# Wide token chunks: a token group moved between the first step's products, one addition per turn moved to GpSimd, the last step in another order

## The chip, the cores and the metric

One core of a Trainium2 chip runs the whole program. The metric is the device time of one execution in microseconds; of several executions the median is taken. Before the change it is 2312.31 us (three runs, 2310.08 to 2313.94).

## The reference

Two stages, in fp32, on x of 8 x 3008 x 256 (batch, tokens, channels). The first filters along the tokens: a real FFT over the 3008 tokens, a complex 256 x 256 channel mixing, a soft threshold, and the inverse FFT. The second is a mixer block:

```
X  = rfft(x, axis=1)
Yr = shrink(Xr @ w_r - Xi @ w_i + b_r)      # shrink: sign(v) * max(|v| - 0.01, 0)
Yi = shrink(Xr @ w_i + Xi @ w_r + b_i)
x  = irfft(Yr + 1j*Yi)                      # 8 x 3008 x 256

h   = relu(x.T @ w_tok1) @ w_tok2           # tokens: 3008 -> 256 -> 3008, per batch
u   = x + h.T
out = u + relu(u @ w_ch1) @ w_ch2           # channels: 256 -> 1536 -> 256
```

## The kernel before, in words

The eight batches are worked on in five units (one, one, two, two, two batches). The transforms, the mixing and the token layer of a unit run beside the channel layers of the unit before it, up to about 905 us; this part is the same in both kernels. What is changed lies behind it, in `channel7` (line 1193).

**u in groups.** u is made in token groups of 376 or 470 tokens (four or five sets of 94). `half_u(g, ct)` makes one half of a group, that is one of two 128-channel blocks: six products with the second token weight (tiles gh, gl, wt; `mm3` writes a value as the sum of two fp32r numbers, high and remainder, and takes three products for one), then the products with the inverse transform's tile b, one for each set of 94 tokens, all into one PSUM bank, here bank z. ScalarE copies the bank into uf, the tile that keeps u (line 975). After the second half `load_group` issues two loads for the next group on SP: wt (line 924) and b (line 946), each with one buffer.

**Channel layers in wide chunks.** From unit 1 on the tokens go in chunks of 1024 (the first of a unit has 960 or 896); these are 21 wide chunks, `ns`. In them both channel layers are computed by a seven-product scheme for 2 x 2 blocks (Strassen, in Winograd's form): u is cut in quarters (channel block by token half: u11, u12, u21, u22, which are also the places of the output sums), and each weight in 2 x 2 blocks of 128 x 128. A chunk takes six steps p, each with two of the twelve hidden blocks. A step has seven products of the first layer, N1 to N7, and seven of the second, O1 to O7; each product is three matmuls (`mm3`) with the half chunk's 512 columns moving. The O of a step run in the next step, between that step's N: `step(new, old, beside)` walks a written list of names. TensorE keeps the order that the code writes (class `InOrder`); for the other engines the compiler's scheduler fixes each queue's order when the program is built.

```
ORDER = "O1 N1 N5 O3 N6 N3 N2 N7 O5 O2 N4 O6 O4 O7"   # line 1359
TURN  = "O1 N1 N5 O5 N6 N3 N2 N7 O3 O2 N4 O6 O4 O7"   # the old step was its chunk's last
LAST  = "O1 O5 O3 O2 O6 O4 O7"                        # no new step is left
```

**Banks.** The N use three PSUM banks in turn, X (sx in the profile), W (sw) and Y (sy), and add into them: N1, N6, N7 and N4 use X, N5 and N3 use W, N2 uses Y. Between them ScalarE copies banks out (lines 1245, 1269), VectorE adds across banks (line 1216) and takes maxima with differences (line 1219). From these come the seven operands `op` of the second layer: the high part on ScalarE (line 1249), the remainder on VectorE for b11 and b22 and on GpSimd for the five others (line 1216). N4 waits for VectorE's addition into W to have read X; the next N5 waits for the b22 remainder to have read W.

The O use the banks L1, L5, L6, L7 (tile l), in which the six steps of a chunk add up, and Y (O3, O4) and z (O2), which VectorE empties into uf in every step. So O3 of a step writes Y, VectorE adds it to u12, and only then N2 may write Y.

**The turn.** In a chunk's last step the sums are finished in the step that belongs to the next chunk already. `fin` (tile t) starts as ScalarE's copy of L1; VectorE adds L6 to it (`o6`), VectorE adds fin to u12, VectorE adds L7 to fin (`o7`), GpSimd adds that to u21 and to u22, and `store` issues the chunk's output on SP. Around a turn GpSimd and ScalarE also prepare the next chunk's quarters (`sums_u`, `operand`).

**Where the groups go.** `when` (line 1400) says at which place of which step the half-groups of the next chunk stand. For the second wide chunk (two groups, four halves) they stand behind N1 of step 1 and behind the steps 1, 2 and 3 of the first wide chunk. In the first wide step, which has no old step, nothing stands between the N.

**The end.** The last chunk's last O run with no new step beside them. There o5 adds L5 to u12 and to u22, o3 and o4 empty Y twice, o6 and o7 add fin on VectorE to u12 and u21 and on GpSimd to u22, and L7 to u21 and u22; the output leaves in four stores on SP.

Of the kernel before, what the change touches and what calls it, by code (L numbers as in the profile page):

```python
# [17 lines left out]
B, N, C = 8, 3008, 256  # L18
N1, N2 = 47, 64
# [118 lines left out]
def tile_kernel(ctx: ExitStack, tc: tile.TileContext, io):  # L138
    nc = tc.nc
    V, S, G, PE, DMA, PUT = nc.vector, nc.scalar, nc.gpsimd, nc.tensor, nc.sync, nc.scalar  # L140
# [66 lines left out]
    def mm3(out, wh, wl, xh, xl, start, stop, more=False):  # L207
        PE.matmul(out, lhsT=wh, rhs=xh, start=start, stop=False, skip_group_check=more)  # L208
        PE.matmul(out, lhsT=wh, rhs=xl, start=False, stop=False, skip_group_check=more)  # L209
        PE.matmul(out, lhsT=wl, rhs=xh, start=False, stop=stop, skip_group_check=more)  # L210
# [674 lines left out]
    outv = io["out"].rearrange("(t p) b n -> b p t n", p=128)  # L885
# [3 lines left out]
    for u, bs in enumerate(UNITS):  # L889
        total, at = N * len(bs), 0  # L890
# [15 lines left out]
    for u, at, cw in chunks:  # L906
        mine = []
# [47 lines left out]
                ufs[m] = wc["uf"].tile([128, 2, CW7 if cw > CW else CW], F32, name="uf", bufs=3)  # L955
        return c0, c1, found

    def half_u(g, ct):
        u, b, s0, k = groups[g]
        gh, gl = gts[u]  # L960
        w, b2 = wts[g], b2s[g]
        c0, c1, found = home(g)
        n = c1 - c0
        cs = slice(ct * 128, (ct + 1) * 128)
        pt = wc["banks"]["z"] if "banks" in wc else bank("pu")
        for jt in range(2):
            mm3(pt[:, :n], gh[:, jt, b, cs], gl[:, jt, b, cs], w[:, jt, :n], w[:, 2 + jt, :n], jt == 0, False)
        for s in range(k):
            PE.matmul(pt[:, s * TOKS:(s + 1) * TOKS], lhsT=b2[:, s, cs], rhs=g2[:, 0 if s0 + s == 0 else 1], start=False, stop=s == k - 1)
        if g == 0:  # L970
            us[0] = [wc["wk2"].tile([128, 2, CW], F32R, name=k, bufs=1) for k in ("uh", "ul")] if ct == 0 else us[0]
            S.copy(out=us[0][0][:, ct, :n], in_=pt[:, :n])
        for m, at, cw in found:
            lo, hi = max(at, c0), min(at + cw, c1)
            S.copy(out=ufs[m][:, ct, lo - at:hi - at], in_=pt[:, lo - c0:hi - c0])
        if g == 0:
            V.tensor_tensor(out=us[0][1][:, ct, :n], in0=ufs[0][:, ct, :n], in1=us[0][0][:, ct, :n].bitcast(F32), op=ALU.subtract)
        if ct:
            del wts[g], b2s[g]
# [198 lines left out]
    def left(layer, p, i):  # L1178
        if i in MADE:
            return [wc["ws" if layer == 1 else "ws2"][:, p, MADE[i], k] for k in range(2)]  # L1180
        row, t = KEPT[i]
        if layer == 1:
            return [wc["w1"][:, k, t, (2 * p + row) * 128:(2 * p + row + 1) * 128] for k in range(2)]
        return [wc[name][:, 2 * p + t, row * 128:(row + 1) * 128] for name in ("w2h", "w2l")]
# [8 lines left out]
    def channel7(ns):  # L1193
# [7 lines left out]
        total = {k: ps2.tile([128, 512], F32, tag="l%d" % k, name="l") for k in (1, 5, 6, 7)}  # L1201
        banks = wc["banks"] = {k: bank("s" + k) for k in ("x", "w", "y", "z")}
        coming, pins = {}, {}

        def piece(g, ct):
            def f():
                half_u(g, ct)
                if ct:
                    load_group(g + 1)
            return f  # L1210

        half = NF // 2
        ADD, SUB, MAX = ALU.add, ALU.subtract, ALU.max

        def add(out, in0, in1, eng, op=ADD):
            eng.tensor_tensor(out=out, in0=in0, in1=in1, op=op)  # L1216
# [11 lines left out]
        def two(old, i):  # L1228
            n, p, h, ops = old
            op = ops[SECOND[i]]  # L1230
            if p == half - 1 and (i == 2 or i == 3 and n < ns[-1]):
                mm3(total[{2: 1, 3: 5}[i]][:, :h], *left(2, p, i), op[:, 0], op[:, 1], False, True, True)
            elif i in total:
                mm3(total[i][:, :h], *left(2, p, i), op[:, 0], op[:, 1], p == 0, p == half - 1)
            else:
                mm3(banks["z" if i == 2 else "y"][:, :h], *left(2, p, i), op[:, 0], op[:, 1], True, True)
# [60 lines left out]
        def of_second(old):  # L1297
            n, p, h, ops = old
            u11, u12, u21, u22 = quarters(n)
            L = {k: t[:, :h] for k, t in total.items()}  # L1300
            Y = banks["y"][:, :h]
            last = p == half - 1
            fin = spare(n) if last else None

            def o1(after=None):
                if after:
                    with tc.issue_after(after.ins):
                        S.copy(out=fin, in_=L[1])
                else:
                    S.copy(out=fin, in_=L[1])  # L1310

            def o3():
                add(u12, L[5] if last and n < ns[-1] else Y, u12, V)

            def o4():
                add(u21, Y, u21, V)
                if n == ns[-1] and last:
                    add(u21, fin, u21, V)

            def o5():  # L1320
                if n == ns[-1]:
                    add(u12, L[5], u12, V)
                add(u22, L[5], u22, V)

            def o2():
                add(u11, L[1] if last else banks["z"][:, :h], u11, V)

            def o6():
                add(fin, L[6], fin, V)
                if n == ns[-1]:  # L1330
                    add(u22, fin, u22, G)
                add(u12, fin, u12, V)

            def o7():
                if n == ns[-1]:
                    add(u21, L[7], u21, V)
                    add(u22, L[7], u22, V)
                    return
                add(fin, L[7], fin, V)
                add(u21, fin, u21, G)  # L1340
                add(u22, fin, u22, G)
                store(n)

            found = {("O", 3): o3, ("O", 4): o4, ("O", 2): o2}
            if last:
                found.update({"l1": o1, "l5": o5, ("O", 6): o6, ("O", 7): o7})
            return found

        def store(n, parts=((slice(0, 2), 0), (slice(0, 2), 1))):
            u, at, cw = chunks[n]  # L1350
            h = cw // 2
            uf = us[n][0]
            for t, k in parts:
                for b, bi in enumerate(UNITS[u]):
                    lo, hi = max(at + k * h, b * N), min(at + (k + 1) * h, (b + 1) * N)
                    if lo < hi:
                        DMA.dma_start(out=outv[bi][:, t, lo - b * N:hi - b * N], in_=uf[:, t, lo - at:hi - at])

        ORDER = "O1 N1 N5 O3 N6 N3 N2 N7 O5 O2 N4 O6 O4 O7".split()

        TURN = "O1 N1 N5 O5 N6 N3 N2 N7 O3 O2 N4 O6 O4 O7".split()

        LAST = "O1 O5 O3 O2 O6 O4 O7".split()

        def step(new, old, beside):
            then = of_second(old) if old else {}
# [33 lines left out]
        when = {}  # L1400
        for m in ns[1:]:
            mine = needs[m]
            if m == ns[1]:
                spots = [(ns[0], p) for p in ['N5', 'N7', (1, 'N1'), 1, 2, 3][-2 * len(mine):]]
            elif len(mine) == 2:
                spots = [(m - 2, half - 1), (m - 1, 0), (m - 1, 1), (m - 1, 2)]
            else:
                spots = [(m - 2, half - 2), (m - 2, half - 1), (m - 1, 0), (m - 1, 1), (m - 1, 2), (m - 1, 3)]
            for spot, half_g in zip(spots, [(g, ct) for g in mine for ct in range(2)]):
                when.setdefault(spot, []).append(half_g)  # L1410
        old = None
        for n in ns:
            for p in range(half):
                h = chunks[n][2] // 2
                new = n, p, h, {k: tail.tile([128, 2, CW], F32R, tag="op", name="op", bufs=9)[:, :, :h] for k in ("b11", "b22", "t1", "b21", "t2", "t4", "t3")}
                beside = {}
                if p == half - 1 and n < ns[-1]:
                    beside = {at: [operand(n + 1, k, {'b22': 'b11', 'b21': 't1'}.get(k)) for k in ks] for at, ks in {'N1': ('t1',), 'N5': ('t2',), 'N7': ('b22',), 'O2': ('b21', 't3', 't4')}.items()}
                for at in ("N1",):
                    if (n, (p, at)) in when:  # L1420
                        beside[at] = [piece(*when[n, (p, at)].pop())]
                if not old:
                    beside = {at: [piece(*when[n, at].pop())] for at in ("N5", "N7") if (n, at) in when}
                step(new, old, beside)
                old = new
                if p == half - 2 and n < ns[-1]:
                    sums_u(n + 1)
                    operand(n + 1, "b11", 'b11')()
                for g, ct in when.get((n, p), ()):
                    piece(g, ct)()  # L1430
        step(None, old, {})
        for part in ((0, 1), (1, 1), (1, 0), (0, 0)):
            store(ns[-1], ((slice(part[0], part[0] + 1), part[1]),))

    def run(gen):
        for _ in gen:
# [81 lines left out]
```

## Time and profile before

| what | before |
|---|---|
| median of three runs | 2312.31 us |
| the profiled execution, its own time | 2313.52 us |
| its span | 2311.7 us |
| granted TensorE clock, mean | 0.997 |
| first wide step begins (first product into sx) | 905.57 us |
| turns (VectorE's addition of fin to u12) | 20, the first at 981.42, the last at 2251.00 us |
| GpSimd busy from 917 to 927 / in an ordinary turn, 1449.7 to 1461.6 | 5.35 of 10.0 / 9.19 of 11.9 us |

Lines of the profile read thus: the start in us from the span's start and the duration in us; the engine (PE is TensorE, DVE VectorE, ACT ScalarE, POOL GpSimd, SPq the queue of SyncE, which issues transfers), the line of the kernel, the operation, what it writes and reads (`sx<-ub,w`), its shape, and how many were merged. In brackets stands the idle time of the engine just before, and who ended it. A waits view has one line for each pair: the waiting engine and line, who was waited for, the us in total, how often, and the longest. Matmul ends are modelled, so distances are taken from start to start. Line 134 is that of the `InOrder` helper, so all products of the wide part carry it: they are told apart by their tiles.

### The profile page before, as it was taken

The page shows a single profiled execution, that of the slowest core. Times are in us where ns is not written, and L with a number is a line of the kernel's source. Part 1 is how long each engine was busy: PE and PEld are TensorE (multiplying, and loading weights), DVE is VectorE, ACT ScalarE, POOL GpSimd, SP SyncE. Part 2 cuts the span into 40 slices and gives each one's busy share as a digit, 9 for nine tenths or more (in the row PEclk, how much of TensorE's full clock was granted, in tenths as well). Part 3 has the DMA queues.
Part 4 walks back from the last instruction along what each step waited for, and adds up shares of the span by engine and source line. Part 5 has one row for each costly group of instructions (what it writes and reads, how often), then busy time and mean ns, then how long its engine had stood idle before and what let it go on. Part 6 is the DMA issues. An engine that isn't in the chain of part 4 may idle for free.

```text
span 2311.7 us, 34801 instructions
## 1 busy us (share of the span) xinstructions
PE 2273.6 (98%) x12092; PEld 1974.3 (85%) x12092; DVE 1722.7 (75%) x2812; ACT 1475.5 (64%) x2700; POOL 1374.2 (59%) x1113
## 2 busy tenths in 40 slices
PE   8999999999999999999999999999999999999998
PEld 7879999989989988888988888898888889888876
DVE  7976776677887667777777777777778777777877
ACT  6764454455555445776676777667677766767775
POOL 0000223344554331887787888778788877878885
PEclk9999999999999999999999999999999999999999
DMA  8885565787876542122222212222221122222101
GB/s 213 263 262 155 152 208 180 233 262 246 271 241 212 185 153 85 44 78 69 84 62 69 64 39 65 70 84 62 69 65 44 59 69 85 62 70 64 59 1 37
DMA packets 150958, 277.23 MB, mean 120 GB/s; under 512 B 11077, under 2 KB 95389, under 8 KB 150781
## 3 DMA queue, kind: packets, MB, share of 16 engines
q1 hardware_dynamic: 115106, 208.21, 29.9%
q10 hardware_dynamic: 35675, 66.78, 8.6%
q8 instruction: 96, 1.57, 0.3%
q14 instruction: 81, 0.66, 0.1%
HBM read 177.57 MB, written 97.39 MB: 119 GB/s over the span
## 4 chain that ended last, share of the span: by engine, by line
PE 81%; DVE 11%; DMA 4%; issue 2%; ACT 1%; SPq 1%; POOL 0%; ACTq 0%; DVEq 0%
PE l L134 15%; PE sx L134 14%; PE sz L134 11%; PE sy L134 10%; PE sw L134 7%; PE px L497 3%; PE pm L208 2%; PE pm L210 2%; PE pm L209 2%; DMA raw<-in_wt 2%; PE gp L210 1%; PE gp L208 1%; PE gp L209 1%; DVE ts L1219 1%; DVE ub L160 1%
## 5 line engine op out<-in xcount | busy, mean ns | idle before, releaser
L1216 POOL TENSOR_TENSOR op<-ts,op 128x512 fp32r<-128x512 f32 (+2 forms) x503 | 639.0, 1294 | 278.0 <-ACT op L1249 271.3
L1249 ACT ACTIVATE op<-ts 128x512 fp32r<-128x512 f32 (+2 forms) x504 | 311.2, 619 | 63.2 <-DVE ts L1219 48.5
L1216 DVE TENSOR_TENSOR uf<-sy,uf 128x512 f32<-128x512 f32 (+2 forms) x232 | 156.0, 672 | 222.1 <-PE sy L134 221.8
L134 PE MATMUL l<-op,ws 128*128 128x512 f32 (+2 forms) x1134 | 314.3, 385 | 0.0
L134 PEld LDWEIGHTS l<-op,ws 128*128 128x128 f32 x1134 | 212.9, 188 | 40.2
L1245 ACT ACTIVATE x<-sx 128x512 f32<-128x512 f32 (+2 forms) x252 | 148.8, 590 | 138.6 <-PE sx L134 138.1
L134 PE MATMUL sx<-ub,w 128*128 128x512 f32 (+2 forms) x756 | 211.1, 387 | 1.8 <-DVE ts L1219 1.0
L134 PE MATMUL sx<-ub,ws 128*128 128x512 f32 (+2 forms) x756 | 209.8, 386 | 0.5 <-ACT x L1245 0.5
L161 POOL TENSOR_TENSOR yl<-z,yh 128x512 fp32r<-128x512 f32 x72 | 96.2, 1336 | 125.7 <-ACT yh L158 119.3
L134 PEld LDWEIGHTS sx<-ub,w 128*128 128x128 f32 x756 | 141.3, 188 | 31.5 <-DVE ts L1219 3.2
L134 PEld LDWEIGHTS sx<-ub,ws 128*128 128x128 f32 x756 | 141.8, 188 | 27.9 <-ACT x L1245 0.9
L1216 POOL TENSOR_TENSOR op<-b,op 128x512 fp32r<-128x512 f32 (+2 forms) x126 | 160.9, 1277 | 0.6 <-ACT op L1249 0.2
L1216 DVE TENSOR_TENSOR x<-sw,x 128x512 f32<-128x512 f32 (+2 forms) x126 | 85.7, 680 | 91.5 <-PE sw L134 91.5
L1269 ACT ACTIVATE x<-x 128x512 f32<-128x512 f32 (+2 forms) x126 | 78.6, 624 | 109.5 <-DVE x L1216 109.5
L208 PE MATMUL pm<-wmh,xth 128*128 128x256 f32 x504 | 145.4, 289 | 1.9 <-DVE z L543 1.7
L134 PE MATMUL sy<-op,w2h 128*128 128x512 f32 (+2 forms) x464 | 142.4, 388 | 1.0 <-DVE uf L1216 1.0
L210 PE MATMUL pm<-wmh,xtl 128*128 128x256 f32 x504 | 142.5, 283 | 0.0
L209 PE MATMUL pm<-wml,xth 128*128 128x256 f32 x504 | 142.4, 283 | 0.0
L262 POOL TENSOR_TENSOR sd<-x 120x512 f32<-120x512 f32 x39 | 61.4, 1575 | 135.6 <-DVE xl L161 59.0
L161 POOL TENSOR_TENSOR xtl<-xs,xth 128x256 fp32r<-128x256 f32 x84 | 68.6, 817 | 116.7 <-ACT xth L158 73.0
L161 POOL TENSOR_TENSOR wt<-aw,wt 128x512 fp32r<-128x512 f32 x12 | 15.8, 1317 | 180.6 <-ACT wt L158 180.6
L506 DVE TENSOR_TENSOR xtl<-px,xth 128x512 fp32r<-128x512 f32 x84 | 57.7, 687 | 72.3 <-ACT xth L505 56.2
(225 smaller groups left out, 6671.4 us busy)
## 6 DMA issues: line engine op xcount, KB each, us to landing
wt<-wt_d SPq DMA_DIRECT2D x28, 940.0 KB, 5.5
x<-in_x SPq DMA_DIRECT2D x39, 480.0 KB, 5.7
a<-a_d SPq DMA_DIRECT2D x36, 512.0 KB, 5.7
wt<-ws_d SPq DMA_DIRECT2D x36, 512.0 KB, 4.7
b_d<-bt ACTq DMA_DIRECT2D x36, 512.0 KB, 5.5
a_d<-a ACTq DMA_DIRECT2D x36, 480.0 KB, 4.3
wt<-wt_d SPq DMA_DIRECT2D x21, 752.0 KB, 5.1
b<-b_d SPq DMA_DIRECT2D x32, 480.0 KB, 6.3
```

What stands on the lines that cost most here:

```text
L134: return lambda *args, **kw: self.tc.keep_in_program_order(op(*args, **kw))
L161: lo_eng.tensor_tensor(out=lo, in0=src, in1=hi.bitcast(F32), op=ALU.subtract)
L208: PE.matmul(out, lhsT=wh, rhs=xh, start=start, stop=False, skip_group_check=more)
L209: PE.matmul(out, lhsT=wh, rhs=xl, start=False, stop=False, skip_group_check=more)
L210: PE.matmul(out, lhsT=wl, rhs=xh, start=False, stop=stop, skip_group_check=more)
L262: eng.tensor_tensor(out=sd[:, 0], in0=x[:, 0], in1=x[:, 1], op=ALU.add)
L497: PE.matmul(pt[:, o:o + 128], lhsT=x, rhs=f2cols(2 * kp + ab), start=True, stop=True)
L506: V.tensor_tensor(out=v(xl)[:, 1:], in0=both, in1=v(xh)[:, 1:].bitcast(F32), op=ALU.subtract)
L1216: eng.tensor_tensor(out=out, in0=in0, in1=in1, op=op)
L1245: pins[key] = S.activation(out=t, in_=src, func=func)
L1249: pins[k] = S.activation(out=ops[k][:, 0], in_=v[k] if src is None else src, func=AF.Copy if k[0] == "t" else AF.Relu)
L1269: pins["x2r"] = S.activation(out=v["x2"], in_=v["x2"], func=AF.Relu)
```

## The change

Three edits.

First, the two halves of the second wide chunk's first group. `half_u` and `piece` get an argument: 0 is the six products with the token weight alone, 1 the products with b, the copy and (second half) the loads. The first half now stands behind N5 of the first wide step, the six products of the second half behind N7 of the same step, the rest of the second half behind that step. Step 1 loses what it had. The second group keeps its place, behind steps 2 and 3.

Second, at the 20 turns the addition of fin to u12 in `o6` goes from VectorE to GpSimd. VectorE's addition of L7 to fin, which comes later and writes what GpSimd reads, has to wait for it.

Third, the last step. Its order is O1 O5 O2 O6 O7 O3 O4. O3 adds into L5 and O4 into L7, where before they went through Y. On VectorE go u22 + L5, u11 + L1, fin + L6, u22 + L7, u12 + fin, u12 + L5, u21 + L7; on GpSimd u21 + fin and u22 + fin. The four stores are issued in another order and in turns on SP and on ScalarE's queue.

```diff
-    def half_u(g, ct):
+    def half_u(g, ct, only=None):
...
         pt = wc["banks"]["z"] if "banks" in wc else bank("pu")
-        for jt in range(2):
-            mm3(pt[:, :n], gh[:, jt, b, cs], gl[:, jt, b, cs], w[:, jt, :n], w[:, 2 + jt, :n], jt == 0, False)
+        if only != 1:
+            for jt in range(2):
+                mm3(pt[:, :n], gh[:, jt, b, cs], gl[:, jt, b, cs], w[:, jt, :n], w[:, 2 + jt, :n], jt == 0, False)
+        if only == 0:
+            return
...
-        def piece(g, ct):
+        def piece(g, ct, only=None):
             def f():
-                half_u(g, ct)
-                if ct:
+                half_u(g, ct, only)
+                if ct and only != 0:
                     load_group(g + 1)
             return f
...
-            if p == half - 1 and (i == 2 or i == 3 and n < ns[-1]):
-                mm3(total[{2: 1, 3: 5}[i]][:, :h], *left(2, p, i), op[:, 0], op[:, 1], False, True, True)
+            if p == half - 1 and (i in (2, 3) or i == 4 and n == ns[-1]):
+                mm3(total[{2: 1, 3: 5, 4: 7}[i]][:, :h], *left(2, p, i), op[:, 0], op[:, 1], False, True, True)
...
             def o3():
-                add(u12, L[5] if last and n < ns[-1] else Y, u12, V)
+                add(u12, L[5] if last else Y, u12, V)

             def o4():
+                if n == ns[-1] and last:
+                    add(u21, L[7], u21, V)
+                    return
                 add(u21, Y, u21, V)
-                if n == ns[-1] and last:
-                    add(u21, fin, u21, V)

             def o5():
-                if n == ns[-1]:
-                    add(u12, L[5], u12, V)
                 add(u22, L[5], u22, V)
...
             def o6():
                 add(fin, L[6], fin, V)
-                if n == ns[-1]:
-                    add(u22, fin, u22, G)
-                add(u12, fin, u12, V)
+                add(u21 if n == ns[-1] else u12, fin, u21 if n == ns[-1] else u12, G)

             def o7():
                 if n == ns[-1]:
-                    add(u21, L[7], u21, V)
                     add(u22, L[7], u22, V)
+                    add(u12, fin, u12, V)
+                    add(u22, fin, u22, G)
                     return
                 add(fin, L[7], fin, V)
                 add(u21, fin, u21, G)
                 add(u22, fin, u22, G)
...
-        LAST = "O1 O5 O3 O2 O6 O4 O7".split()
+        LAST = "O1 O5 O2 O6 O7 O3 O4".split()
...
             if m == ns[1]:
-                spots = [(ns[0], p) for p in ['N5', 'N7', (1, 'N1'), 1, 2, 3][-2 * len(mine):]]
+                assert len(mine) == 2
+                g = mine[0]
+                when.update({(m - 1, "N5"): [(g, 0)], (m - 1, "N7"): [(g, 1, 0)], (m - 1, 0): [(g, 1, 1)]})
+                when.update({(m - 1, 2): [(mine[1], 0)], (m - 1, 3): [(mine[1], 1)]})
+                continue
...
-                for at in ("N1",):
-                    if (n, (p, at)) in when:
-                        beside[at] = [piece(*when[n, (p, at)].pop())]
...
-                for g, ct in when.get((n, p), ()):
-                    piece(g, ct)()
+                for part in when.get((n, p), ()):
+                    piece(*part)()
         step(None, old, {})
-        for part in ((0, 1), (1, 1), (1, 0), (0, 0)):
-            store(ns[-1], ((slice(part[0], part[0] + 1), part[1]),))
+        for part, queue in (((0, 0), DMA), ((0, 1), PUT), ((1, 0), DMA), ((1, 1), PUT)):
+            store(ns[-1], ((slice(part[0], part[0] + 1), part[1]),), queue)
```

More of the change, by code (lines that the diff above doesn't have):

```diff
@@ L1347, in of_second, with store @@
             return found
-        def store(n, parts=((slice(0, 2), 0), (slice(0, 2), 1))):
+        def store(n, parts=((slice(0, 2), 0), (slice(0, 2), 1)), queue=DMA):
             u, at, cw = chunks[n]
@@ L1356, in store @@
                     if lo < hi:
-                        DMA.dma_start(out=outv[bi][:, t, lo - b * N:hi - b * N], in_=uf[:, t, lo - at:hi - at])
+                        queue.dma_start(out=outv[bi][:, t, lo - b * N:hi - b * N], in_=uf[:, t, lo - at:hi - at])
         ORDER = "O1 N1 N5 O3 N6 N3 N2 N7 O5 O2 N4 O6 O4 O7".split()
         TURN = "O1 N1 N5 O5 N6 N3 N2 N7 O3 O2 N4 O6 O4 O7".split()
-        LAST = "O1 O5 O3 O2 O6 O4 O7".split()
+        LAST = "O1 O5 O2 O6 O7 O3 O4".split()
         def step(new, old, beside):
```

## The prediction

> **What bounds the kernel now.** I read the page first, then the waits from 905 us on (the wide chunks), then the timelines of the first wide step, of two ordinary turns, of the last turn and of the end.
>
> ```profile
> PE 2273.6 (98%) x12092; PEld 1974.3 (85%) x12092; DVE 1722.7 (75%) x2812; ACT 1475.5 (64%) x2700; POOL 1374.2 (59%) x1113
> PE sy L134 <- DVE uf L1216: 2.4, 4, 1.4
> ```
>
> TensorE is busy 98% of the span, and from 905 us it runs back to back: the second line says that in 1400 us it waited 2.4 us, in 4 times, for VectorE's additions into uf. An edit to VectorE or GpSimd can therefore win time only where TensorE is not fed. There are three such places: the first wide step, the turn into the last chunk, and the end. At all other places the same edit can only cost.
>
> The first wide step has no earlier step whose second-layer products (O) could stand between its first-layer products (N), which run in the order N1 N5 N6 N3 N2 N7 N4. TensorE's rows, from N1 of step 0 to N5 of step 1:
>
> ```profile
> 905.57 0.82 PE L134 MATMUL sx<-ub,w 128*128 128x480 f32 x3
> 906.23 0.81 PE L134 MATMUL sw<-ub,ws 128*128 128x480 f32 x3
> 907.56 0.91 PE L134 MATMUL sx<-ub,ws 128*128 128x480 f32 x3 [0.52 <-ACT x L1245]
> 911.18 0.92 PE L134 MATMUL sx<-ub,w 128*128 128x480 f32 x3 [0.76 <-DVE sw L1216]
> 913.72 0.92 PE L134 MATMUL sx<-ub,w 128*128 128x480 f32 x3 [0.63 <-DVE ts L1219]
> 914.47 0.59 PE L134 MATMUL sz<-wt,gh 128*128 128x470 f32 x2
> 915.75 1.25 PE L134 MATMUL sz<-g,b 96*128 96x94 f32 x10
> 916.79 0.90 PE L134 MATMUL sw<-ub,ws 128*128 128x480 f32 x3
> ```
>
> The reader is to see three waits (for a copy by ScalarE, then twice for VectorE) and the first half of the token group at 914.47. A product takes 0.66 us from start to start (906.23 less 905.57). The half-group takes 2.32 (916.79 less 914.47): 1.28 for its six wide products and 1.04 for the products with b. From 905.57 to 916.79 are 11.22 us; nine products and one half-group are 9 x 0.66 + 2.32 = 8.26. About 3.0 us are lost.
>
> **Change, first step.** The first half now stands behind N5, the six products of the second half behind N7, its products with b behind N4; step 1 keeps neither. If nothing waits, N5 of step 1 starts at 905.57 + 9 x 0.66 + 2 x 2.32 = 916.15, and step 1 is 2.32 shorter: 0.64 + 2.32 = 2.96 saved. What may now be late is VectorE's chain behind N7:
>
> ```profile
> 909.61 0.81 PE L134 MATMUL sx<-ub,ws 128*128 128x480 f32 x3
> 910.46 0.67 DVE L1216 TENSOR_TENSOR sw<-sx,w 128x480 f32<-128x480 f32 x1
> 914.14 0.65 DVE L1219 SCALAR_TENSOR_TENSOR op<-sw,op 128x480 fp32r<-128x480 f32 x1
> 900.62 0.31 SPq L946 DMA_DIRECT2D b<-b_d  x1
> b<-b_d SPq DMA_DIRECT2D x1, 480.0 KB, 6.5
> ```
>
> From the addition into W to the end of the b22 remainder, which frees W for the next N5, are 914.14 + 0.65 - 910.46 = 4.33 us. N7 now starts at 905.57 + 5 x 0.66 + 2.32 = 911.2 and the addition 0.85 later, as before (910.46 against 909.61), so W is free at 916.4 at the latest: a new wait of 0.2 at N5. I take **2.8 saved**. Covers: the group's b tile lands at 900.62 + 6.5 = 907.1, and its first use moves to 906.9 + 1.3 = 908.2; the wt tile is issued on the same queue ahead of it. The eviction of the first half on ScalarE stands behind the two copies and ahead of N6's copy, whose product comes after it anyway. The two loads of the next group move about 11 us forward on SP, past no other transfer. If the chain took the whole of what N7 is put off by (2.32 - 0.85), 1.4 would be left; the other end is 2.96.
>
> **Change, ordinary turns (19).** At a turn the old chunk's kept sum (fin, tile t) is added into u12. This goes from VectorE to GpSimd; VectorE's next addition into fin must then wait for GpSimd to have read it.
>
> ```profile
> L1216 DVE TENSOR_TENSOR uf<-t,uf x22: 678/1095/2420, 981.4 to 2306.5; 128x512 f32<-128x512 f32 x18, 128x448 f32<-128x448 f32 x3, 128x480 f32<-128x480 f32 x1
> 1451.95 2.54 POOL L1216 TENSOR_TENSOR uf<-t,uf 128x512 f32<-128x512 f32 x2
> 1450.94 0.69 DVE L1216 TENSOR_TENSOR t<-l,t 128x512 f32<-128x512 f32 x1
> 1452.24 0.69 DVE L1216 TENSOR_TENSOR uf<-sy,uf 128x512 f32<-128x512 f32 x1 [0.60 <-PE sy L134]
> 1453.67 0.69 DVE L1216 TENSOR_TENSOR x<-sw,x 128x512 f32<-128x512 f32 x1 [0.74 <-PE sw L134]
> 1454.96 0.70 DVE L1216 TENSOR_TENSOR sw<-sx,w 128x512 f32<-128x512 f32 x1
> 1456.12 0.84 PE L134 MATMUL sx<-ub,w 128*128 128x512 f32 x3
> 984.84 2.41 POOL L1216 TENSOR_TENSOR uf<-t,uf 128x480 f32<-128x480 f32 x2
> 986.48 0.70 DVE L1216 TENSOR_TENSOR sw<-sx,w 128x512 f32<-128x512 f32 x1
> 987.63 0.84 PE L134 MATMUL sx<-ub,w 128*128 128x512 f32 x3
> ```
>
> VectorE gets back 1.1 us, the median of the first row, but TensorE waits for nothing here: the gain is nil. The cost: GpSimd is free of its remainders at 1451.95 and ends the addition at 1453.2. Then fin += L7, before at 1450.94, can start. Between 1452.93 and 1453.67 VectorE is idle, so it takes 0.2 to 0.3 of the busy time after it, and W's addition ends at 1455.9, ahead of N4 at 1456.12: no wait. In the turn of the last three rows GpSimd is free only at 984.84; fin += L7 takes W's place at 986.48, W is ready at 987.8 instead of 987.2, and N4 waits 0.2. I count seven of the nineteen turns as this kind (here and where the step runs 0.4 ahead; an estimate from such rows): **1.2 lost**, ends 0 and the rival below. GpSimd's own 1.3 us more per turn falls into a gap: after its two additions to 1454.5 its next work waits for the coming step's operands. The chunk's stores leave SP some 2.5 us later; nobody waits for them.
>
> **Change, last turn.** Here no token group follows, and TensorE does wait.
>
> ```profile
> 2249.09 3.78 POOL L1216 TENSOR_TENSOR op<-ts,op 128x512 fp32r<-128x512 f32 x3
> 2251.00 2.42 DVE L1216 TENSOR_TENSOR uf<-t,uf 128x512 f32<-128x512 f32 x1
> 2254.13 0.68 DVE L1216 TENSOR_TENSOR uf<-sy,uf 128x512 f32<-128x512 f32 x1
> 2252.67 0.84 PE L134 MATMUL sw<-ub,w 128*128 128x512 f32 x3
> 2254.86 0.97 PE L134 MATMUL sy<-ub,w 128*128 128x512 f32 x3 [1.35 <-DVE uf L1216]
> ```
>
> VectorE's addition from fin took 2.42 instead of 0.68: it ends 0.55 behind GpSimd's run (2252.87). The addition out of Y comes two places after it, at 2254.13, and N2 (2254.86) waits for that. With the kept sum on GpSimd, VectorE is free at 2251.0. O3's product ends at about 2252.2 (N6 and N3 follow it, 0.68 each), Y is empty 0.7 later, at 2252.9, and N2 starts 0.68 behind N3, at 2253.35: 1.5 won, 0.1 given back at N4 as in a late turn: **1.4 won**, ends 0 and 1.5.
>
> **Change, the end.**
>
> ```profile
> 2299.71 0.84 PE L134 MATMUL l<-op,ws 128*128 128x512 f32 x3
> 2300.27 0.57 ACT L1310 COPY t<-l 128x512 f32<-128x512 f32 x1
> 2300.75 0.97 DVE L1216 TENSOR_TENSOR op<-ts,op 128x512 fp32r<-128x512 f32 x1
> 2301.65 1.27 DVE L1216 TENSOR_TENSOR uf<-l,uf 128x512 f32<-128x512 f32 x2
> 2305.24 1.97 DVE L1216 TENSOR_TENSOR uf<-t,uf 128x512 f32<-128x512 f32 x2
> 2307.32 1.29 DVE L1216 TENSOR_TENSOR uf<-l,uf 128x512 f32<-128x512 f32 x2
> 2308.67 0.33 SPq L1357 DMA_DIRECT2D out<-uf  x1
> ```
>
> VectorE sets the end: eleven operations with hardly a gap from 2300.75 to 2308.61, and the last store follows at 2308.67. The change makes eight of them: O3 and O4 accumulate into L5 and L7, which saves one addition each, and u21 + fin goes to GpSimd. In the new order O1 O5 O2 O6 O7 O3 O4, O2 waits for ScalarE's copy out of L1 (2300.27 + 0.57 = 2300.84); O6 and O7 follow 0.68 apart, O7 ending at 2303.1. VectorE starts an addition each 0.6: the remainder at 2300.75, then u22, u11, fin and u22 from 2301.65 to 2304.1. O4 may overwrite L7 then and ends at 2305.0. The one addition left with both inputs in SBUF, u12 + fin, meets GpSimd's u21 + fin (2303.5 to 2304.8), and ends at 2305.45; u12 + L5 and u21 + L7 follow to 2306.65, beside GpSimd's u22 + fin. The last addition ends 1.9 earlier, and the stores, now on two queues, do not line up: **1.9 won**. The ends: 2.8 if nothing is held up, and 0.7 if u12 + fin is held through both of GpSimd's additions, as the 2.42 us row was held past the end of the operation that ran when it began (2251.0; three in 3.78 us, so a border at 2251.6). The median of the 22 such additions is 1.1, which is a wait to the next border; I take that.
>
> The Trainium skill ("SBUF — State Buffer", "SBUF: two separate sides") calls the port pair of VectorE and GpSimd an exclusive lock, held for a whole instruction by whichever starts first. By it u12 + fin would wait for one of GpSimd's additions and the end would win 1.9 and the sum stay 4.9. The 2.42 us row waited longer than one instruction, so this trace agrees only in part; by that row the end wins 0.7 and the sum is 3.7.
>
> **Sum.** 2.8 + 1.4 + 1.9 - 1.2 = 4.9 us. The profiled execution took 2313.5 and would take 2308.6; the median of the three runs is 2312.3, 1.2 below it, and I predict 2312.3 - 4.9 = **2307.4**.
>
> **Rivals.** (A) VectorE's queue is fixed when the program is built. If fin += L7 stands in it ahead of the next step's addition out of Y (as in the rows at 1450.94 and 1452.24), VectorE stops until GpSimd is done at 1453.2, Y is empty at 1454.6, and N2, due four products of 0.68 ahead of N4 (1453.40), waits 1.2. Late turns wait 2.5 (GpSimd done at 986.05, Y empty at 987.4, N2 due at 984.9), those that run ahead 1.7: 12 x 1.2 + 4 x 2.5 + 3 x 1.7 = 29.5. The last turn (GpSimd done at 2254.1, Y empty at 2255.5) then loses 0.7 instead of winning 1.4: 2312.3 + 29.5 + 0.7 - 2.8 - 1.9 = **2338**, slower. It decides from 0.3 us per turn on. Against it:
>
> ```profile
> 2236.93 0.69 DVE L1216 TENSOR_TENSOR uf<-sy,uf 128x512 f32<-128x512 f32 x1
> 2237.90 0.69 DVE L1219 SCALAR_TENSOR_TENSOR ts<-sx,ts 128x512 f32<-128x512 f32 x1 [0.28 <-POOL op L1216]
> ```
>
> Here the code writes the second row's operation first; the queue has them the other way round, and the one moved back still waits for GpSimd. So the order goes by what is expected to be ready, GpSimd's delay included. Chance 0.12. (B) The end is held through both GpSimd additions and the last turn's wait only moves to another product: 2312.3 - 2.8 - 0.7 + 1.2 = **2310.0**. The 2.42 us row speaks for it. Chance 0.23. (C) The first step is bound by the chain ScalarE to VectorE, not by missing work, and N5 waits as long as the half-group that was put ahead: 1.4 won there, 2312.3 - 1.4 - 1.4 - 1.9 + 1.2 = **2308.8**. For it: all three waits are for that chain. Against: two of them end while the pieces run. Chance 0.15. My forecast keeps 0.5.
>
> **Numbers.** The three runs lie 3.9 us apart (0.17%: 2310.08 to 2313.94), so 0.2%, 4.6 us, is about what can be told from none; its borders are 2307.7 and 2316.9. The bounds add up to 7.3 won (2.96 + 1.5 + 2.8 - 0) and 0.9 won (1.4 + 0 + 0.7 - 1.2); with 1.5 us for the run they give 2303.5 to 2312.9, which holds the forecast, B and C and leaves out A. Faster: three quarters of the forecast, a third of C and a tenth of B, 0.45; slower: A and a little, 0.13; the same, 0.42.
>
> **What would show it.** In the changed profile: no wait over 0.3 in the first step and its next N5 near 916.3; no N2 wait at any turn, and the last turn's 1.35 gone; the kept sum's row on GpSimd with three additions a turn; the last addition near 2306.7 less the gain before. A row "PE sy <- DVE uf" with some twenty waits of over 1 us would make me wrong by A; a group at the first step that waits for its tiles would make me wrong there.

## The result and the profile after

The changed kernel takes 2337.27 us (median of four runs, 2336.94 to 2341.23), the kernel before beside it 2311.19 (four, 2308.18 to 2313.94): ratio 1.0112, 95% interval 1.0099 to 1.0124. It is 26 us slower; 2307.4 had been forecast, with 2303.5 to 2312.9 as the range. The profiled execution took 2341.23, its span is 2339.4.

The page of the changed kernel, busy times, and its waits from 900 to 2340 us (waiting engine, whom it waits for: us in total, times, the longest):

```profile
PE 2283.4 (98%) x12092; PEld 1978.2 (85%) x12092; DVE 1697.0 (73%) x2789; ACT 1473.9 (63%) x2700; POOL 1392.7 (60%) x1134
```

```profile
DVE t L1219 <- POOL uf L1219: 63.8, 20, 4.2
PE sy L134 <- DVE uf L1219: 19.7, 21, 1.9
```

TensorE's share of busy time is the same 98%, and would have told nothing. The two waits tell it: VectorE stands still for GpSimd once at each of the 20 turns, 63.8 us in all, and TensorE waits for VectorE 21 times before a product into Y (N2 at each of the 20 turns, and one O3), where it had waited 4 times for 2.4 us. That is the row that the prediction named as the mark of rival A, though most of its waits are shorter than the 1 us named there. The timeline of the changed kernel shows an ordinary turn (first eight rows), a late one, and the last one:

```profile
1458.78 3.78 POOL L1219 TENSOR_TENSOR op<-ts,op 128x512 fp32r<-128x512 f32 x3
1460.18 0.68 DVE L1219 TENSOR_TENSOR uf<-sy,uf 128x512 f32<-128x512 f32 x1
1462.52 1.29 POOL L1219 TENSOR_TENSOR uf<-t,uf 128x512 f32<-128x512 f32 x1
1463.06 0.84 PE L134 MATMUL sx<-ub,ws 128*128 128x512 f32 x3
1463.74 0.84 PE L134 MATMUL sw<-ub,w 128*128 128x512 f32 x3
1463.84 0.69 DVE L1219 TENSOR_TENSOR t<-l,t 128x512 f32<-128x512 f32 x1 [2.99 <-POOL uf L1219]
1464.45 0.68 DVE L1219 TENSOR_TENSOR uf<-sy,uf 128x512 f32<-128x512 f32 x1
1465.19 0.96 PE L134 MATMUL sy<-ub,w 128*128 128x512 f32 x3 [0.61 <-DVE uf L1219]
...
988.27 0.66 DVE L1219 TENSOR_TENSOR t<-l,t 128x480 f32<-128x480 f32 x1 [4.15 <-POOL uf L1219]
989.58 0.97 PE L134 MATMUL sy<-ub,w 128*128 128x512 f32 x3 [1.87 <-DVE uf L1219]
...
2282.12 0.69 DVE L1219 TENSOR_TENSOR t<-l,t 128x512 f32<-128x512 f32 x1 [3.03 <-POOL uf L1219]
2283.46 0.96 PE L134 MATMUL sy<-ub,w 128*128 128x512 f32 x3 [1.89 <-DVE uf L1219]
```

Read it along VectorE. After its addition out of Y at 1460.18 the next thing in its queue is fin += L7 (`t<-l,t`). That writes the tile which GpSimd, busy with its remainders, reads only from 1462.52 to 1463.81. VectorE stops for 2.99 us. Behind it in the queue stands the next step's addition out of Y (1464.45), which had had its input since 1463.2, when O3's product ended, and behind that N2. N2 was due 0.68 after 1463.74 and starts 0.77 late. At the late turn it is 2.0 late and at the last one 2.1, and the product behind each N2 comes a further 0.12 late (N2 takes 0.96 to start up instead of 0.84). From N2 to N2 this adds up to 22.6 us, with the 0.12 of 20 turns to 25.0; before, the one such wait, at the last turn, cost 1.5.

The first wide step of the changed kernel:

```profile
909.55 0.82 PE L134 MATMUL sx<-ub,w 128*128 128x480 f32 x3
912.14 1.25 PE L134 MATMUL sz<-g,b 96*128 96x94 f32 x10
913.42 0.55 ACT L978 COPY uf<-sz 128x470 f32<-128x470 f32 x1 [2.40 <-PE sz L134]
913.87 0.58 ACT L1248 ACTIVATE x<-sx 128x480 f32<-128x480 f32 x1
914.33 0.58 ACT L1248 ACTIVATE w<-sw 128x480 f32<-128x480 f32 x1
914.50 0.92 PE L134 MATMUL sx<-ub,ws 128*128 128x480 f32 x3 [1.11 <-ACT x L1248]
921.79 0.92 PE L134 MATMUL sw<-ub,ws 128*128 128x480 f32 x3
```

ScalarE's copy out of Z, for which it waits 2.40 us, stands ahead of the copies of x and w, though X and W were full at 910.4 and 911.0. N6 (914.50) waits 1.11 for X. From N1 to N5 of step 1 are 12.24 us with both halves of the group, against 11.22 with one: 11.22 + 2.32 - 12.24 = 1.3 saved.

The end of the changed kernel, and the time that its last three stores took from issue to landing:

```profile
2327.60 0.61 PE L134 MATMUL l<-op,w2h 128*128 128x512 f32 x2
2332.19 2.95 POOL L1219 TENSOR_TENSOR uf<-t,uf 128x512 f32<-128x512 f32 x2 [0.72 <-DVE t L1219]
2332.63 1.39 DVE L1219 TENSOR_TENSOR uf<-t,uf 128x512 f32<-128x512 f32 x1
2334.13 1.29 DVE L1219 TENSOR_TENSOR uf<-l,uf 128x512 f32<-128x512 f32 x2
2335.18 0.83 ACTq L1358 DMA_DIRECT2D out<-uf  x2
```

```profile
DMA to landing us min/median/max: 2.0/2.4/3.0
```

VectorE's last addition ends 7.82 us after O1 (2335.42 less 2327.60), before it was 9.58: 1.76 earlier. But O1 to the end of the span is 11.8 against 12.7: 0.9 won. The rest went into the stores: three of them leave within 0.5 us and land 2.0, 2.4 and 3.0 us later. Before, they left 0.6 apart at the closest and each landed in 2.0 to 2.1. One of the three left late by its place in a queue, too: u12 was done at 2334.82 (the first of the two additions that begin at 2334.13), but on ScalarE's queue its store stands behind that of u22, which waits for GpSimd until 2335.14 (2332.19 + 2.95). The row at 2335.18 holds both: u22's store first, u12's at 2335.61.

**A ruler.** The span's start is not a good mark: the code up to 905 us is the same in all kernels here, and yet the first wide product came between 900.8 and 909.6 us. So the profiles are compared from that product to the end of the span. Before: 2311.7 - 905.57 = 1406.1. After: 1429.9, 23.8 more. That is the 25.0 of the turns less the 1.5 of before, less 1.3 in the first step and 0.9 at the end, which makes 21.3. The granted clock adds to it: it is 0.91 in two stretches of 20 us (1600 to 1620 and 2000 to 2020), and from N2 to the next N2 TensorE takes 13.20 there against 11.61 behind the two other late turns, 1.6 us each time. Both stretches begin right behind a late turn's wait (last section), so I count these 3.2 us with the same cause. That makes 24.5, 0.7 more than measured; three steps away from the turns are 0.2 to 0.3 shorter than before, and why is open.

### The profile page after: what moved, and what is told of

It reads as the page before. It is cut to its first block, busy times and chain, and to the rows that moved or that the text cites. A ratio compares the mean times of both kernels' runs of the same rounds, so it can differ in the third digit from the quotient of the medians.

```text
span 2339.4 us, 34775 instructions
## 1 busy us (share of the span) xinstructions
PE 2283.4 (98%) x12092; PEld 1978.2 (85%) x12092; DVE 1697.0 (73%) x2789; ACT 1473.9 (63%) x2700; POOL 1392.7 (60%) x1134
## 4 chain that ended last, share of the span: by engine, by line
PE 76%; DVE 10%; POOL 4%; DMA 4%; issue 2%; ACT 2%; SPq 1%; ACTq 0%; DVEq 0%; POOLq 0%
PE l L134 13%; PE sx L134 13%; PE sy L134 9%; PE sz L134 9%; PE sw L134 6%; POOL op L1219 3%; PE px L497 3%; PE pm L208 2%; PE pm L210 2%; PE pm L209 2%; DMA raw<-in_wt 1%; PE gp L208 1%; PE gp L210 1%; PE gp L209 1%; POOL uf L1219 1%
## 5 line engine op out<-in xcount | busy, mean ns | idle before, releaser
L1219 POOL TENSOR_TENSOR op<-ts,op 128x512 fp32r<-128x512 f32 (+2 forms) x503 | 629.4, 1273 | 269.6 <-ACT op L1252 266.0
L134 PE MATMUL sy<-ub,w 128*128 128x512 f32 (+2 forms) x378 | 107.2, 392 | 19.3 <-DVE uf L1219 19.3
```

Source lines behind the costliest of these rows:

```text
L134: return lambda *args, **kw: self.tc.keep_in_program_order(op(*args, **kw))
```

## The experiments

My theory: VectorE's wait for GpSimd, by its place in VectorE's queue, is the whole loss. Rivals: GpSimd's additional work as such (the summed 1.3 us a turn makes it the bound), or a loss in the first step or the end.

| kernel | median us (runs) | ratio to before, 95% interval | first wide product to end, us |
|---|---|---|---|
| before (with e1 to e4) | 2310.99 (27) | | 1406.1 |
| after | 2337.27 (4) | 1.0112, 1.0099 to 1.0124 | 1429.9 |
| e1 kept sum on VectorE | 2308.23 (11) | 0.9992, 0.9983 to 1.0001 | 1403.5 |
| e2 turn alone | 2337.53 (4) | 1.0117, 1.0103 to 1.0131 | 1433.8 |
| e3 own tile | 2306.50 (11) | 0.9982, 0.9973 to 0.9991 | 1401.0 |
| e4 wait later in the queue | 2310.44 (11) | 1.0001, 0.9990 to 1.0012 | 1405.6 |
| before (with e5 to e8) | 2311.36 (24) | | |
| e5 own tile, copy behind | 2305.11 (8) | 0.9968, 0.9958 to 0.9979 | 1399.7 |
| e6 first step alone | 2309.71 (11) | 0.9991, 0.9983 to 1.0000 | 1403.8 |
| e7 end alone | 2312.78 (11) | 1.0006, 0.9997 to 1.0014 | 1407.7 |
| e8 written later | 2334.36 (2) | 1.0100, 1.0082 to 1.0119 | 1429.9 |
| before (with e9, e10) | 2310.89 (11) | | |
| e9 e5 with one queue | 2302.86 (6) | 0.9963, 0.9951 to 0.9976 | 1400.2 |
| e10 e5 with three stores | 2304.69 (1) | | 1399.1 |

**e1** puts the one addition back on VectorE and keeps the rest of the change:

```
-add(u21 if n == ns[-1] else u12, fin, u21 if n == ns[-1] else u12, G)
+add(u21 if n == ns[-1] else u12, fin, u21 if n == ns[-1] else u12, G if n == ns[-1] else V)
```

> The changed kernel with the turn's addition of the kept sum back on VectorE; the first step and the end stay as changed. Theory (the loss is VectorE's wait for GpSimd at the 20 turns, 1.1 us of idle TensorE at each): the wait for GpSimd goes, no N2 waits at an ordinary turn, about 2309, 2 below before. Rival 1 (the loss is GpSimd's longer load, whatever waits): about 2309 too, so this run does not part it from the theory. Rival 2 (the first step or the end loses): 2320 or more.

Measured 2308.23. The waits for GpSimd are gone, and with them the 26 us: the first step and the end cannot be where the time went. N6's wait of 1.1 in the first step is still there. The 2.6 us that it is ahead of the kernel before by the ruler are 1.3 in the first step and 1.3 at the last turn, whose wait is nearly gone although the addition is back on VectorE (last section); its end, 12.7 us from O1, has won nothing.

**e2** makes the kernel before with this one edit alone:

```
-add(u12, fin, u12, V)
+add(u12, fin, u12, G if n < ns[-1] else V)
```

> The kernel before with only the turn's addition moved to GpSimd. Theory and rival 1: some 20 waits of TensorE at N2, before + 23, 2334. Rival 2: no more than before + 5, 2316.

Measured 2337.53, as slow as the whole change. Its waits, 900 to 2340 us:

```profile
DVE t L1216 <- POOL uf L1216: 63.8, 20, 4.2
PE sy L134 <- DVE uf L1216: 20.4, 23, 1.9
```

To the tenth the same 63.8 us in 20 waits. One edit makes the loss, alone and in company.

**e3** leaves the addition on GpSimd and takes away the reason to wait: the sum with L7 goes into another tile, so that nothing overwrites what GpSimd still reads.

```
-add(fin, L[7], fin, V)
-add(u21, fin, u21, G)
-add(u22, fin, u22, G)
+fin2 = spare(n)
+add(fin2, L[7], fin, V)
+add(u21, fin2, u21, G)
+add(u22, fin2, u22, G)
```

> The changed kernel, but VectorE writes fin + L7 to a tile of its own, so it need not wait until GpSimd has read fin; GpSimd still makes three additions a turn. Theory: all N2 waits go, the last turn's too; 2307.5, some 4 below before. Rival 1 (GpSimd's load): the loss stays, 2330 or more. Rival 2: 2337.

Measured 2306.50, ratio 0.9982. GpSimd does the same work (busy 1391.7 us in e3's page, 1392.7 after), so its load is not the cause. The last turn of e3 in the timeline:

```profile
2244.14 3.84 POOL L1219 TENSOR_TENSOR op<-ts,op 128x512 fp32r<-128x512 f32 x3
2246.09 0.68 DVE L1219 TENSOR_TENSOR t<-l,t 128x512 f32<-128x512 f32 x1
2247.29 0.69 DVE L1219 TENSOR_TENSOR uf<-sy,uf 128x512 f32<-128x512 f32 x1 [0.52 <-PE sy L134]
2247.78 0.85 PE L134 MATMUL sw<-ub,w 128*128 128x512 f32 x3
2248.47 0.84 PE L134 MATMUL sy<-ub,w 128*128 128x512 f32 x3
```

The sum with L7 runs at 2246.09, while GpSimd is still in its remainders; VectorE then waits for O3's product, not for GpSimd, and N2 follows N3 by 0.69. This is the turn as the prediction had drawn it.

**e4** keeps the tile and the wait, and puts the waiting instruction behind the next step's addition out of Y in VectorE's queue:

```
+pins["y"] = add(u12, L[5] if last else Y, u12, V)      # in the next step's O3
...
-add(fin, L[7], fin, V)
-add(u21, fin, u21, G)
-add(u22, fin, u22, G)
-store(n)
+def rest():                                            # written behind the next step's O3
+    with tc.issue_after(pins["y"].ins):                # an order edge: not ahead of that addition
+        add(fin, L[7], fin, V)
+    add(u21, fin, u21, G)
+    add(u22, fin, u22, G)
+    store(n)
+held.append(rest)
```

> The changed kernel with VectorE's addition of L7 to fin put behind the next step's addition out of Y in VectorE's queue; the tile and GpSimd's work are as changed. Theory with the queue's order as the cause: N2 no longer waits; VectorE's wait for GpSimd shrinks to under 1 us at most turns and up to 2 at the late ones, where N4 may wait 0.2 to 1; 2309 to 2315. If the wait only moves to the next product, it stays above 2330. Rival 1: 2330 or more.

Measured 2310.44, ratio 1.0001. The waits of e4:

```profile
DVE t L1219 <- POOL uf L1219: 7.3, 8, 1.2
PE sx L134 <- DVE sw L1219: 1.9, 5, 0.4
```

The wait shrinks from 63.8 to 7.3 us, and N2's is gone. What remains is of the kind that the forecast had priced: at the four late turns and the last one N4 waits up to 0.4 for W. Here the queue has the order that the prediction assumed. It is still about 4 us behind e3 (2310.44 against 2306.50; 1405.6 against 1401.0 by the ruler), more than the 1.9 us of waits that this row shows. From start to start the cost is larger: behind O2's last products N4 starts after 0.75 to 0.80 us instead of e3's 0.23, the products behind it start slowly too, and each of these five steps takes 0.7 to 1.0 longer than in e3, 3.9 in all.

**e8** asks what sets that order. It is e4 without the order edge: the three additions and the store are written in the program behind the next step's O3, and nothing else holds them there:

```
-add(fin, L[7], fin, V)
-add(u21, fin, u21, G)
-add(u22, fin, u22, G)
-store(n)
+def rest():
+    add(fin, L[7], fin, V)
+    add(u21, fin, u21, G)
+    add(u22, fin, u22, G)
+    store(n)
+held.append(rest)
...
+if new and name == "O3" and held:
+    held.pop()()
```

> The changed kernel with the addition of L7, GpSimd's two additions and the store written in the program behind the next step's O3 instead of behind O7, with no wait or edge added. Theory (each queue's order goes by when the compiler's scheduler expects an operation to be ready, and it expects GpSimd to be done sooner than it is): the addition of L7 still stands ahead of the addition out of Y in VectorE's queue, N2 waits at some twenty turns and the time is about 2337. Rival (the queue follows the order of the program's lines): the waits go, as in e4, about 2310.

Measured 2334.36, and again the row of after, to the tenth:

```profile
DVE t L1219 <- POOL uf L1219: 63.8, 20, 4.2
```

The place of the lines does not set the order of the queue, and the edge alone makes the difference between e8's 63.8 us and e4's 7.3. That the order goes by an estimate in which GpSimd is done sooner than it is fits this; the estimate itself was not seen.

**e5** takes e3 and puts, in the first step, the copy out of Z behind the copies of x and w on ScalarE, as it stands in the kernel before:

```
+first = beside["N5"][0]      # first half of the group and its copy
...
+with tc.issue_after(pins["w1"].ins):
+    first()
...
+beside["N5"] = [behind]      # behind: the function that holds the two lines above
```

> The changed kernel with L7's addition writing a tile of its own (as in e3) and, in the first wide step, the copy of the token group's first half put on ScalarE's queue behind the copies of x and w, where the kernel before has it. Theory (the first step saved only 1.3 of the 2.8 us because ScalarE held the copies of x and w back behind the copy out of Z): N6's wait of 1.1 us goes, N1 of step 0 to N5 of step 1 falls from 12.2 to about 11.1 us, and the time is 1.1 below e3's, about 2305.4. Rival (the first step is bound by the chain of ScalarE and VectorE, rival C): the wait moves to N7 or N5 and the time stays within 0.4 of e3's 2306.5.

Measured 2305.11, ratio 0.9968. Its first step:

```profile
904.79 0.82 PE L134 MATMUL sx<-ub,w 128*128 128x480 f32 x3
908.40 0.89 PE L134 MATMUL sx<-ub,ws 128*128 128x480 f32 x3
908.66 0.55 ACT L978 COPY uf<-sz 128x470 f32<-128x470 f32 x1 [1.47 <-PE sz L134]
915.67 0.93 PE L134 MATMUL sw<-ub,ws 128*128 128x480 f32 x3
```

N6 starts 3.61 after N1 (4.95 in the changed kernel) and waits for nothing; N1 to N5 is 10.88: 11.22 + 2.32 - 10.88 = 2.66 saved. The order of one copy in ScalarE's queue was worth 1.36 us. By the times alone (1.4 below e3, intervals that overlap) this would not be decided; by the rows it is.

**e6 and e7** make the kernel before with the first edit alone and with the edit of the end alone.

> The kernel before with the first of the three edits alone (the token group in three parts, behind N5, behind N7 and behind N4). Theory: what the changed kernel's rows show, one half-group less in step 1 and a new wait of 1.1 at N6, so 1.3 us faster than before, ratio about 0.9994, and no waits at the turns. Rival (the wait at N6 comes from something else that the change moved): no wait there and 2.8 us faster, ratio 0.9988.

> The kernel before with the edit of the end alone (L5 and L7 take O3 and O4, the order O1 O5 O2 O6 O7 O3 O4, the last stores on two queues, the kept sum's additions of the last step on GpSimd). Theory, from the changed kernel's rows: the last step from O1 to the end of the span falls from 12.7 to 11.8 us, 0.9 faster, ratio 0.9996; VectorE's last addition ends 1.7 us earlier after O1 and the last store lands later after it. Rival (my prediction's step): 1.9 faster, ratio 0.9992.

e6 measured 2309.71, ratio 0.9991; N1 to N5 is 12.23, as after, so 1.3 of the 2.4 us by the ruler (1406.1 less 1403.8) come from the first step. The other part was not expected: the last turn's wait of 1.35 is gone, though that turn was not edited. e7 measured 2312.78, ratio 1.0006: no gain that can be told from none. Its clock was at 0.91 from 900 to 920 us, which cost 1.6 us in the first step (N1 to N5 12.78 instead of 11.22; in the ruler too); O1 to the end is 12.6, only 0.1 less than before, with VectorE done 1.8 earlier. Its last three stores:

```profile
DMA to landing us min/median/max: 2.0/3.3/3.8
```

The last landed 0.8 later after its issue than in the changed kernel. The DMA view of e7's last 5 us has a row that those of the changed kernel, e3, e4, e5 and e8 (3.0 for the last) do not have:

```profile
q14 instruction: 1, 0.01, 0.4%
```

It is one transfer of 8 KB, begun at 2309.01, in the middle of the three stores. In e1, with the same last stores, one began at 2303.28, and the last landed after 3.8 as well. That it holds them up fits these seven kernels; no run tests it. (The kernel before and e6 have one too, at 2308.4 and 2302.4, and their stores, 0.6 apart, landed in at most 2.1 and 2.3.)

**e9 and e10** ask why the stores give VectorE's gain back. Both are e5; e9 has the last stores all on SP's queue, e10 leaves the last of them out.

```
-for part, queue in (((0, 0), DMA), ((0, 1), PUT), ((1, 0), DMA), ((1, 1), PUT)):
+for part, queue in (((0, 0), DMA), ((0, 1), DMA), ((1, 0), DMA), ((1, 1), DMA)):    # e9
+for part, queue in (((0, 0), DMA), ((0, 1), PUT), ((1, 0), DMA)):                   # e10
```

> e5 with all four of the last stores on SP's queue, as the kernel before has them. Theory (the end won 0.9 at best instead of 1.9 because the changed order lets the last three stores leave within 0.5 us on two queues, where they land 2.0, 2.4 and 3.0 us after their issue, or 2.0, 3.3 and 3.8, against 2.0 to 2.1 when they leave 0.7 apart on one): one queue sets them 0.35 apart, the last of them lands in 2.1 to 2.5, and O1 to the end of the span stays at 11.8 us or falls by up to 0.4; the time is within 0.5 of e5's 2305.1. Rival (two queues are worth having): the issues line up on SP and the end is 0.5 or more later, 12.3.

> e5 without the last of the stores (u22 of the last chunk, a quarter of its output, is not stored). Theory (the last three stores hold each other up): the two that are left land in 2.0 to 2.5 us and the span ends 0.5 to 1.7 us sooner after O1, at 11.0 to 11.3. Rival (a store that leaves last lands last for other reasons, such as a fixed cost after the last addition): it ends where it did, 11.8.

The four stores of e9, and the three of e10:

```profile
DMA to landing us min/median/max: 2.0/2.2/2.5
```

```profile
DMA to landing us min/median/max: 2.0/2.0/2.1
```

With one store fewer the others land in 2.0 to 2.1 again and the end comes 10.8 us after O1 (2302.9 less 2292.09), 1.0 sooner than in e5: stores that leave close together do hold each other up. The last store of e10 leaves 7.9 after O1 against e5's 8.0, so nearly all of this is landing time. Without the store of u22, that of u12 leaves as soon as it is ready, 0.6 ahead of the last, so the run does not part the number of stores from their distance. What they share shows in e5's DMA view: for the 2 us in which the three stores of 256 KB move, the 16 DMA engines are over 80% busy at 310 to 410 GB/s. With one queue they leave 0.45 to 0.47 apart, the last at 2298.8, and land in at most 2.5; O1 to the end is 11.9, e5's 11.8: one queue or two, the end is where it was. e9's median, 2302.86, is 2.2 below e5's, but the kernel before beside it is lower too and the ruler has e9 0.5 longer: its ratio, 0.9963, cannot be told from e5's 0.9968. Both beat the kernel before by about a third of a per cent.

## Why the prediction was wrong

**The bound** was read rightly: TensorE runs back to back, an edit to VectorE or GpSimd can only cost at an ordinary turn, and it did.

**Ordinary turns: the step that failed.** The prediction had fin += L7 behind the addition out of Y, where it "takes 0.2 to 0.3 of the busy time". On the chip it stands ahead of that addition. The sum had the turns at 1.2 us; they and the last one cost some 27 (by the ruler, 1429.9 less e1's 1403.5 is 26.4, with the last stores of e1 0.9 later; by the rows 25.0 in the waits of N2 and behind them and 3.2 by the clock, 0.9 more than measured). The term was too small in the order that it assumed, too: in e4 the four late turns cost 0.7 each, 2.9 in all, where the prediction had 0.2 for each of seven. The mechanism was in the prediction as rival A, at a chance of 0.12. What told against it was one pair of rows (2236.93 and 2237.90), from which the prediction drew that the queue's order goes by readiness, "GpSimd's delay included". e8 bears out that the written order does not set it; that GpSimd's real delay is in it is what fell. In the pair the instruction moved back still had to wait 0.28 for GpSimd, which could have been read as a delay estimated too short.

**Rival A's price** came out at 2338 for 2337.27, partly by luck. It had 1.2 us at an ordinary turn (0.77 measured), 2.5 at a late one (2.0), the gains of the first step and the end too large, and nothing of the clock. The reason for the first: with VectorE's addition gone, nothing cuts into GpSimd's three remainders, which take 3.78 us (1458.78) instead of the 4.23 of ordinary turns before, so GpSimd is done sooner.

**First step: 2.8 forecast, 1.3 measured.** The step that failed is the cover "the eviction of the first half on ScalarE stands behind the two copies". It stood ahead of them and held both back. With that order put right, e5 saves 2.66; the rest of the working (one half-group and all three waits filled, N5 0.2 late) was right, and rival C falls.

**Last turn: 1.4 forecast, lost in the changed kernel, won in e3.** There the row at 2248.47 follows N3 without a wait: 1.5 won. In e4 the last turn wins the same 1.5 and its next step loses 0.8, so 0.1 for N4 was too little. But e1 and e6, which leave the addition on VectorE, win 1.3 here as well: the wait was not firm, and starts a few hundredths of a us apart went two ways (below).

**The end: 1.9 forecast, 0.9 measured at best (0 to 0.1 in e1 and e7).** VectorE's part was right to a tenth and a half (1.76; u12 + fin took 1.39 and got in between GpSimd's two additions, as assumed, so the hold of rival B did not come). The step that failed is "the stores, now on two queues, do not line up". They line up in ScalarE's queue, where u12's waits behind u22's, and again while they move. The Trainium skill ("DMA: Bandwidth & Descriptors", "Issuing engines are not separate DMA queues") says that transfers issued by different engines run on the same 16 DMA engines and interleave; the landings of 2.0, 2.4 and 3.0 us, and e10's 2.0 to 2.1 with a store fewer, agree with it. Here three results that became ready within 0.6 us were stored no sooner for having two queues (e5 against e9); what u12's store ahead of u22's would win was not run.

## What to carry to other kernels

Moving an operation to another engine turns the next write of its input into a wait across engines; before pricing that wait, ask where in the waiting engine's queue it stands and what ready work is held behind it, since 1.3 us of GpSimd's work cost nothing here (e3) and its place in VectorE's queue cost about 1.3 us a turn. Look at every queue that the change touches: ScalarE's copy in the first step and its store of u12 stood behind a waiting instruction in the same way. Where the order of a queue isn't known, give the wait nothing to wait for (another tile, e3) or fix the order (e4). A faster last computation wins only what the last stores leave: look at when they leave and how long they take to land, not at when the engine is done.

## What the runs showed of the hardware

**Starts a few hundredths of a us apart went two ways at the last turn.** VectorE's addition with both inputs in SBUF met GpSimd's three remainders at the last turn of e6 and of e7 alike (a border is the place where one of GpSimd's operations ends and the next begins):

```profile
2244.21 4.23 POOL L1219 TENSOR_TENSOR op<-ts,op 128x512 fp32r<-128x512 f32 x3
2246.18 1.11 DVE L1219 TENSOR_TENSOR uf<-t,uf 128x512 f32<-128x512 f32 x1
```

```profile
2249.30 3.80 POOL L1216 TENSOR_TENSOR op<-ts,op 128x512 fp32r<-128x512 f32 x3
2251.22 2.42 DVE L1216 TENSOR_TENSOR uf<-t,uf 128x512 f32<-128x512 f32 x1
```

In e6 it starts 1.97 us after GpSimd's run, is let in at the next border (1.11 us) and GpSimd's run grows to 4.23; in e7 it starts 1.92 after, is passed over and waits for the run's end (2.42), as in the kernel before (1.91 after, 2.42). In e1 it starts 1.95 after and is let in (1.13). At the other turns of full width, where it starts 1.99 to 2.00 after, it takes 1.08 to 1.10. The time to the border alone does not decide it: at three late turns of the kernel before the addition, 448 columns wide there, starts 0.63 or 0.64 ahead of the first border and is let in (1.11 to 1.12); at the last turn it starts 0.62 ahead of the second and is passed over. The Trainium skill ("SBUF — State Buffer", "SBUF: two separate sides") has the pair held for the instruction that came first; a wait past a border, which these rows show, is more than that. e1 and e6 have the first edit, e7 and the kernel before do not; how it moves the start by some 0.05 us at the far end of the kernel is open.

**The clock can drop behind waits of 1.9 us.** The windows view of the changed kernel around the late turn whose N2 starts at 1598.93 (busy time of each engine, then the granted clock, the share of the DMA engines and GB/s):

```profile
1598.00:1600.00 2.00, 1.07 (x5) 0.89 (x6) 1.54 (x4) 0.49 (x1) 1.64 (x2) 1.00 0.00 0
1600.00:1602.00 2.00, 2.00 (x6) 1.59 (x5) 1.62 (x3) 0.94 (x3) 0.60 (x1) 0.50 0.79 289
1602.00:1604.00 2.00, 2.00 (x7) 1.60 (x6) 1.92 (x4) 0.96 (x2) 0.96 (x1) 0.64 0.45 169
1604.00:1606.00 2.00, 2.00 (x10) 1.65 (x10) 1.31 (x3) 1.65 (x3) 0.68 (x2) 1.00 0.00 0
```

TensorE waited 1.86 us, went on at 1598.93, and from about 1600 to 1603.5 has half its clock: six and seven matmuls in 2 us instead of ten. The changed kernel, e2 and e8 have fifteen waits of 1.85 to 1.91 us (four late turns and the last one each); seven of them are followed by such a stretch within 2 us, the others by none, and between 940 and 2280 us no kernel without these waits has one. A wait that is followed by one costs a further 1.6 us, and the same place is hit in one run and not in another. The clock's record shows which. The stretches of one run begin a multiple of 3.41 us apart, those before 905 us included (2009.62 less 1600.02 is 120 times 3.413). On that grid each of the seven waits lies between two marks (1597.07 to 1598.93, marks at 1596.60 and 1600.02), and each of the eight others lies across one (1188.65 to 1190.51, mark at 1190.42). That is a pattern of fifteen cases; no run moved a wait to test it. One such stretch also stands in e7's first wide step, from 912.5 on, behind two waits of 0.76 and 0.62. The Trainium skill ("TensorE: Matmul & The Clock Gate", "HAM oscillation — how this bites in real kernels") warns of idle gaps of more than about 3.4 us; here 1.9 were enough in seven cases of fifteen, and the measurement decides.
